# A fused attention, soft-MoE and MLP kernel: steps of the attention stage put at other places of the program

## The chip, the cores and the metric

The kernel runs on one core of a Trainium2 chip. A core has five engines, each with its own in-order instruction stream: TensorE (matmuls and transposes), VectorE, ScalarE, GpSimd and SyncE, whose queue here issues nearly all DMA transfers. Engines wait for each other by semaphores. The metric is the device time of one execution in microseconds (us), the median of the runs.

## What is computed

Rotary attention over 32 heads, a soft mixture of experts, and a gated MLP, all in 32 bit precision:

```python
def _attn_ref(q, k, v):                       # (4, 8, 576, 64)
    ...
    q_rot, k_rot = (rotate(q), rotate(k))
    scores = scale * np.matmul(q_rot, k_rot.transpose(0, 1, 3, 2))
    scores = scores - np.max(scores, axis=-1, keepdims=True)
    attn = np.exp(scores)
    attn = attn / (np.sum(attn, axis=-1, keepdims=True) + 1e-09)
    return np.matmul(attn, v).astype(np.float32)

def _moe_ref(x, phi, w1, w2):                 # x (2304, 512), 8 experts, 32 slots
    logits = x @ phi
    ...                                       # d: softmax over the tokens
    slot_input = d.T @ x
    ...                                       # two layers with relu for each expert's slots
    ...                                       # c: softmax of the logits over the slots
    return (c @ slot_out).astype(np.float32)

def _moe2_ref(x, w_in, w_out):                # 512 -> 2048 -> 512
    h = x @ w_in
    g = h * (1.0 / (1.0 + np.exp(-h)))
    return (g @ w_out).astype(np.float32)
```

## The kernel before

The kernel has an attention stage (up to about 361 us), the experts' two layers, and the MLP. The change is in the attention stage alone.

**Groups, pairs, places.** The 32 heads are taken as 16 pairs. A pair p has ten groups, numbered g = 10 p to 10 p + 9: for each half of the queries (288 of 576), five chunks of keys in the order 4, 0, 1, 2, 3. This text calls g - 10 p the place. In a group TensorE makes the scores of one chunk for both heads (L392/L393 at places 0 and 5, else L403/L404), ScalarE takes their exponential (L394, L405), and TensorE multiplies exponentials of the five groups before with the values (`pv`, L429, L432) at places 0 and 5, and at places 2 and 7 together with their sums (`sums`, L441, L443).

**The row maxima.** While pair p runs, nine units (L351) find the maxima of a later pair p + 2 from half-differences: TensorE makes two tiles `psmx`, ScalarE a relu (L356), VectorE a reduction (L365, into `mx`). A unit stands in each place except place 5: units 0 to 3 at places 6 to 9, units 4 to 8 at places 0 to 4 of the next pair. They need `kd`, the key difference (`k_diff`, L340, VectorE), and the operand tiles. When all nine are done, TensorE transposes `mx` (`max_rows`, L373, at place 5), ScalarE copies it (L378), and SyncE sends it into row 64 of `qb` (L379), which the scores of the pair need from its place 0 on.

**Rotary.** The queries and keys of a pair are loaded (`load`, L230), multiplied by the tables on VectorE (f0, L275) and GpSimd (f1, L278), added (f2, L281), rounded on ScalarE (f3, L285), and the rest subtracted (f4, L290), each once for both heads. SyncE then spreads the halves to the operand tiles: `m0` (three transfers, L294, waits for f3), `m1` (two, `sa` and `kb`, waits for f4), `m2` (L310, to `qb`).

**Batches of tokens.** Four pairs make a batch. Each pair's output `xt` (`norm2`, L461) is transposed in two parts (`x_t`, L473; ScalarE evicts them, L477 to L483), and a batch has the steps logits (L495), logits2 (L500), soft, expo (the exponential, L508), d_t (transposes L515 and copies L517/L518 into `d` and `lt`), s_mm (sums of the slots, L526/L529, copied by ScalarE, L530).

**PSUM.** `ps_st` has three buffers (scores, logits), `ps_mx` three (units), `ps_u` one (products), and `ps_m` one for the sums, the maxima, the transposes of x, d_t and s_mm in turn.

**Weights.** Loads of the experts' weights (`load_w`, L138) and the narrowing of the MLP's 64 bit weights go on beside it: `fetch` (L142) loads, `conv` narrows (ScalarE L152, VectorE L155, L158), `keep` (L653, L654) stores.

**What sets the order.** A table of tasks, filled by hand-set numbers. After the matmuls of a group, its tasks run in the order in which they were put in; a number is relative to the pair's first group, so -24 for pair p is place 6 of pair p - 3:

```python
for o, k, a in ROTARY:
    at(g0 + o[min(p, 5) - 2], rt(p, k, *a))
at(g0 + V_LOAD, lambda p=p: load_v(p))
first(g0 + (K_DIFF_2, K_DIFF_3, K_DIFF_4, K_DIFF)[min(p, 5) - 2], lambda p=p: k_diff(p))
...
at(g0 + X_T[p % 4][i], lambda p=p, i=i: x_t(p, i))
...
at(gc - FETCH_AHEAD, lambda i=i: fetch(i))
```

The order thus made is each engine's order; an engine does not wait for a group to end, only for the semaphores of its next instruction.

Of the kernel before, what the change touches and what calls it, by code (L numbers as in the profile page):

```python
# [38 lines left out]
ROT_2 = (-26, -22, -19, -21, -23, -19, -19, -18, -18, -18, -17, -18, -17)  # L39
ROT_3 = (-31, -25, -27, -26, -26, -24, -23, -23, -22, -16, -22, -19, -15)  # L40
ROT_4 = (-28, -28, -26, -28, -24, -23, -23, -20, -22, -17, -19, -21, -17)
ROT = (-31, -30, -30, -28, -26, -25, -24, -23, -22, -21, -22, -21, -20)
Q_COPY = -6
V_LOAD = -6
K_DIFF_2 = -14
K_DIFF_3 = -15
K_DIFF_4 = -16
K_DIFF = -17
QK_LOAD = -35
QK_LOAD_3 = -54  # L50
QK_LOAD_4 = -31
# [3 lines left out]
MAX_ROW_3 = -5  # L55
RECIP = 7
NORM = 7
X_T = ((21, 26), (16, 21), (16, 21), (16, 21))
W_IN_AT = (10, 20, 30, 40, 49, 60, 70, 81, 89, 100, 110, 120)
W_IN_STEPS = (1, 1, 5)  # L60
FETCH_AHEAD = 5
BATCH = (14, 16, 20, 21, 22, 23, 26, 30)
W_LOADS = (34, 54, 64, 75, 66, 84, 86, 76, 105, 95, 118, 130, 126, 143, 127, 137, 136, 138, 145, 155)
SCALES = -19
W_OUT_EARLY = (3, 6, 9, 12)
W_OUT_AT = ((0, 122, 130, 133), (1, 135, 139, 143))
# [10 lines left out]
def attn_softmoe_mlp_kernel(ctx: ExitStack, tc: tile.TileContext, qk, v, cst, phi, w1, w2, w_in, w_out, out):  # L77
# [119 lines left out]
    with tc.manual_schedule():  # L197
        with ExitStack() as t1:
# [37 lines left out]
            def load_v(p):  # L236
                t = (ops_c, p2)[p % 2].tile([128, 5, 128], F32, tag="v", bufs=1, name=f"v{p}")
                (act if p == NPAIR - 1 else sp).dma_start(out=t, in_=v[p])
                vt[p] = t
# [96 lines left out]
            def k_diff(p, heads=slice(0, 2)):  # L336
                ka = operands(p)[1]
                k = bass.AP(tensor=ka.tensor, offset=ka.offset, ap=[(W2, 128), (640, 2), (1, S)]).bitcast(F32)[:, heads]
                kd_of[p % 2] = p
                dve.tensor_tensor(out=kds[p % 2][:, heads], in0=k[:, :, 0:HS], in1=k[:, :, HS:S], op=ALU.subtract)  # L340
# [294 lines left out]
            def at(g, *fs):  # L635
                tasks.setdefault(g, []).extend(fs)

            def first(g, f):
                tasks.setdefault(g, []).insert(0, f)
# [23 lines left out]
            def rt(p, k, *a):  # L663
                return lambda: begin(p) if k == 8 else rot[p][k](*a)
# [3 lines left out]
            def begin_batch(b):  # L668
                bt[b] = batch(b)
# [3 lines left out]

            ROTARY = [([r[i] for r in (ROT_2, ROT_3, ROT_4, ROT)], k, a) for i, (k, a) in enumerate(((8, ()), (0, (0,)), (1, (0,)), (1, (1,)), (0, (1,)), (2, (0,)), (2, (1,)), (3, (0, act)), (3, (1, act)), (5, ()), (4, (0,)), (4, (1,)), (6, ())))]

            for p in range(NPAIR):
# [3 lines left out]
                if p >= 2:  # L680
# [4 lines that stand above are left out]
                if p >= 3:  # L685
# [12 lines left out]
                for i in range(2 * (p < NPAIR - 1)):  # L698
                    at(g0 + X_T[p % 4][i], lambda p=p, i=i: x_t(p, i))
                if p % 4 == 3 and p < NPAIR - 1:  # L700
                    b = p // 4
                    at(g0 + BATCH[0], lambda b=b: begin_batch(b), bf(b, 0, 0))
                    at(g0 + BATCH[1], bf(b, 0, 1))
                    at(g0 + BATCH[2], bf(b, 1, 0))
                    at(g0 + BATCH[3], bf(b, 1, 1))
                    at(g0 + BATCH[4], bf(b, 2))
                    at(g0 + BATCH[5], bf(b, 3))
                    at(g0 + BATCH[6], bf(b, 4))
                    at(g0 + BATCH[7], bf(b, 5))
            for i in range(12):  # L710
                gc = W_IN_AT[i]
                at(gc, lambda i=i: conv(i), lambda i=i: cv[i][0]())
# [23 lines left out]
            for i in range(NWA + 4):  # L736
                at(W_LOADS[i], lambda i=i: load_w(i))
            at(10 * NPAIR + SCALES, scales)
# [505 lines left out]
```

## Time and profile before

| | |
|---|---|
| runs | 629.95, 635.74, 639.93 us; median 635.74 |
| profiled execution | 634.98 us, of which the profile's span is 633.2 us |
| busy: TensorE, VectorE, ScalarE, GpSimd | 587.9, 407.0, 359.8, 233.6 us |
| mean granted clock of TensorE | 0.975 |
| DMA | 113.86 MB, mean 180 GB/s |

The profile is of one execution. PE is TensorE, PEld its weight loads (they overlap PE), DVE is VectorE, ACT ScalarE, POOL GpSimd, SP SyncE. A row of the timeline has start, duration, engine, line, operation, tiles (buffer numbers left out) and shapes, and in brackets the idle time of the engine before it and what ended it.

### The profile page before, as it was taken

The page shows a single profiled execution, that of the slowest core. Times are in us where ns is not written, and L with a number is a line of the kernel's source. Part 1 is how long each engine was busy: PE and PEld are TensorE (multiplying, and loading weights), DVE is VectorE, ACT ScalarE, POOL GpSimd, SP SyncE. Part 2 cuts the span into 40 slices and gives each one's busy share as a digit, 9 for nine tenths or more (in the row PEclk, how much of TensorE's full clock was granted, in tenths as well). Part 3 has the DMA queues.
Part 4 walks back from the last instruction along what each step waited for, and adds up shares of the span by engine and source line. Part 5 has one row for each costly group of instructions (what it writes and reads, how often), then busy time and mean ns, then how long its engine had stood idle before and what let it go on. Part 6 is the DMA issues. An engine that isn't in the chain of part 4 may idle for free.

```text
span 633.2 us, 10521 instructions
## 1 busy us (share of the span) xinstructions
PE 587.9 (93%) x3571; PEld 421.4 (67%) x3571; DVE 407.0 (64%) x865; ACT 359.8 (57%) x920; POOL 233.6 (37%) x195
## 2 busy tenths in 40 slices
PE   5768799999999999999989999799899999999997
PEld 3545467766676766765666434577788888888886
DVE  6687678888798887895643433678755544454452
ACT  3446467776776767775665331588664443444342
POOL 5365548767578566773453000312300000000000
PEclk9678889999999999998999999999999999999999
DMA  6885769977789986878959899734202000020002
GB/s 214 206 216 162 201 145 281 246 217 239 212 231 303 303 245 200 226 237 225 297 199 365 297 389 394 277 122 152 85 1 93 8 0 1 2 100 1 0 1 99
DMA packets 43188, 113.86 MB, mean 180 GB/s; under 512 B 4976, under 2 KB 6272, under 8 KB 41344
## 3 DMA queue, kind: packets, MB, share of 16 engines
q1 hardware_dynamic: 42956, 112.87, 58.3%
q8 instruction: 28, 0.46, 0.3%
q10 hardware_dynamic: 180, 0.34, 0.2%
q14 instruction: 24, 0.20, 0.1%
HBM read 78.12 MB, written 7.60 MB: 135 GB/s over the span
## 4 chain that ended last, share of the span: by engine, by line
PE 70%; ACT 11%; DVE 8%; DMA 7%; issue 3%; SPq 0%; POOL 0%; ACTq 0%; DVEq 0%
PE ops L1186 9%; PE ops L1184 9%; PE ops L1185 9%; PE u L432 8%; PE psmx L351 5%; PE st L403 4%; PE st L404 3%; PE s L441 3%; PE l L926 3%; DMA w_in_raw<-in_w_in_dram 3%; PE hps L1079 2%; PE u L429 2%; PE s L443 2%; PE l L905 2%; ACT e L405 2%
## 5 line engine op out<-in xcount | busy, mean ns | idle before, releaser
L405 ACT ACTIVATE e<-st 128x288 f32<-128x288 f32 x256 | 104.4, 419 | 30.3 <-PE st L404 27.6
L1184 PE MATMUL ops<-wo_hi,ghi 128*128 128x512 f32 x288 | 112.8, 392 | 0.0
L1186 PE MATMUL ops<-wo_hi,glo 128*128 128x512 f32 x288 | 112.4, 390 | 0.0
L1185 PE MATMUL ops<-wo_lo,ghi 128*128 128x512 f32 x288 | 112.4, 390 | 0.0
L1086 DVE TENSOR_TENSOR hps<-hps,g 128x384 f32<-128x384 f32 x96 | 49.8, 561 | 84.4 <-ACT g L1083 84.0
L1083 ACT ACTIVATE g<-hps 128x384 f32<-128x384 f32 x96 | 42.3, 490 | 81.9 <-PE hps L1079 81.6
L403 PE MATMUL st<-sa,sa 128*128 128x288 f32 x256 | 85.9, 337 | 0.2
L365 DVE CUSTOM_DVE_ANT_0 relu<-psmx,relu 128x288 f32<-128x288 f32 x144 | 64.4, 449 | 30.8 <-ACT relu L356 22.6
L417 POOL TENSOR_TENSOR es<-e,e 128x576 f32<-128x576 f32 x31 | 46.5, 1499 | 98.9 <-ACT e L405 98.9
L432 PE MATMUL u<-e,v 128*64 128x288 f32 x512 | 79.9, 430 | 0.0
L404 PE MATMUL st<-qb,kb 65*128 65x288 f32 x256 | 76.2, 299 | 0.0
L403 PEld LDWEIGHTS st<-sa,sa 128*128 128x128 f32 x256 | 49.2, 192 | 23.9 <-issue 14.9
L356 ACT ACTIVATE relu<-psmx 128x288 f32<-128x288 f32 x144 | 60.1, 420 | 8.6 <-PE psmx L351 6.2
L1186 PEld LDWEIGHTS ops<-wo_hi,glo 128*128 128x128 f32 x288 | 54.1, 188 | 11.4
L278 POOL TENSOR_TENSOR raw<-raw,tab 128x576 f32<-128x576 f32 x31 | 54.9, 1776 | 17.4 <-DMA sa<-sa 8.1
L1185 PEld LDWEIGHTS ops<-wo_lo,ghi 128*128 128x128 f32 x288 | 54.1, 188 | 10.0 <-issue 0.4
L1184 PEld LDWEIGHTS ops<-wo_hi,ghi 128*128 128x128 f32 x288 | 54.1, 188 | 9.9 <-issue 0.2
L432 PEld LDWEIGHTS u<-e,v 128*64 128x64 f32 x512 | 36.6, 141 | 31.3 <-issue 16.4
L351 PE MATMUL psmx<-sa,sa 128*128 128x288 f32 x160 | 48.3, 319 | 9.0 <-DVE mx L365 7.4
L422 POOL TENSOR_TENSOR es<-es,e 128x576 f32<-128x576 f32 x31 | 53.8, 1734 | 4.8 <-ACT e L405 3.5
L1092 DVE TENSOR_TENSOR glo<-hps,ghi 128x384 fp32r<-128x384 f32 x96 | 49.4, 551 | 4.9 <-ACT ghi L1089 1.8
L351 PE MATMUL psmx<-kd,sa 128*128 128x288 f32 x160 | 47.4, 313 | 5.2 <-DVE kd L340 4.1
(197 smaller groups left out, 1024.8 us busy)
## 6 DMA issues: line engine op xcount, KB each, us to landing
w<-in_w_dram SPq DMA_DIRECT2D x64, 512.0 KB
sa<-raw SPq DMA_DIRECT2D x56, 288.0 KB
raw<-in_qk_dram SPq DMA_DIRECT2D x13, 1152.0 KB
w_out_raw<-in_w_out_dram SPq DMA_DIRECT2D x16, 512.0 KB
w_in_raw<-in_w_in_dram SPq DMA_DIRECT2D x12, 512.0 KB
v<-in_v_dram SPq DMA_DIRECT2D x15, 320.0 KB
qb<-sa SPq DMA_DIRECT2D x16, 288.0 KB
out_dram<-os SPq DMA_DIRECT2D x18, 256.0 KB
```

Of the source, the lines that this page charges most:

```text
L278: eng.tensor_tensor(out=r[:, hd, 1], in0=r[:, hd, 1], in1=c(1), op=ALU.mult)
L351: pe.matmul(t, lhsT=rem_cols(qa, hd, 128) if u == 4 else qa[:, c0:c0 + 128], rhs=k, start=u != 4 or hd == 0, stop=u != 4 or hd == 1)
L356: act.activation(out=r, in_=t, func=ACTF.Relu)
L365: dve.tensor_tensor_reduce(out=r, in0=mxt.pop((p, u, 1)), in1=r, scale=1.0, scalar=-3.0e38, op0=ALU.add, op1=ALU.max, accum_out=mx[p][:, u ...
L403: pe.matmul(st, lhsT=ka[:, c0:c0 + 128], rhs=qa[:, o:o + HS], start=True, stop=False)
L404: pe.matmul(st, lhsT=kb[0:65, c0:c0 + 128], rhs=qb[0:65, S * hd + HS * h:S * hd + HS * h + HS], start=False, stop=True)
L405: act.activation(out=e[:, hd], in_=st, func=ACTF.Exp, scale=0.125)
L422: add(out=es[p, h], in0=es[p, h], in1=e, op=ALU.add)
L432: pe.matmul(u_ps[p, h][64 * hd:64 * hd + 64, :], lhsT=vt[p][:, c, 64 * hd:64 * hd + 64], rhs=e[:, hd], start=False, stop=c == 3, skip_grou ...
L1184: pe.matmul(t, lhsT=a, rhs=wo_hi[k], start=k == 0, stop=False)
L1185: pe.matmul(t, lhsT=a, rhs=wo_lo[k], start=False, stop=False)
L1186: pe.matmul(t, lhsT=b, rhs=wo_hi[k], start=False, stop=k == 15)
```

## The change

The diff changes numbers of the tables alone:

```diff
-ROT = (-31, -30, -30, -28, -26, -25, -24, -23, -22, -21, -22, -21, -20)
+ROT = (-31, -30, -30, -28, -26, -24, -24, -23, -21, -21, -20, -21, -20)
-V_LOAD = -6
+V_LOAD = -5
-K_DIFF = -17
+K_DIFF = -16
-X_T = ((21, 26), (16, 21), (16, 21), (16, 21))
-W_IN_AT = (10, 20, 30, 40, 49, 60, 70, 81, 89, 100, 110, 120)
+X_T = ((21, 26), (14, 21), (16, 19), (16, 20))
+W_IN_AT = (12, 20, 30, 40, 50, 58, 70, 81, 89, 100, 110, 120)
-BATCH = (14, 16, 20, 21, 22, 23, 26, 30)
-W_LOADS = (34, 54, 64, 75, 66, 84, 86, 76, ...)
+BATCH = (16, 16, 20, 21, 22, 25, 26, 29)
+W_LOADS = (34, 54, 64, 76, 66, 82, 86, 76, ...)
```

`ROT` and `K_DIFF` hold from pair 5 on. The entries of `ROT` are begin, f0 head 0, f1 head 0, f1 head 1, f0 head 1, f2 head 0, f2 head 1, f3 head 0, f3 head 1, m0, f4 head 0, f4 head 1, m1: f2 of head 0 and f3 of head 1 go one group later, f4 of head 0 two. `V_LOAD` holds from pair 2 on. `X_T` has the two parts of a batch's first to fourth pair. `BATCH` has, after logits of half 0 and 1, logits2 of half 0 and 1, soft, expo, d_t and s_mm. `W_IN_AT` has the groups in which twelve pieces are converted (the fetch is five groups earlier), `W_LOADS` those in which weight pieces 0 to 19 are loaded.

TensorE's order at places 4 to 6 of pair 10 shows the transposes `xps` of pairs 8 and 9, the first two of a batch (`st` are scores, the second number after the pair is the half, then the chunk or `r` for chunk 4, then the head). Before, at place 6:

```order
L373 MATMUL psm11_3088<-cst_sb_73,mx11_2841 9x128
L403 MATMUL st10_1_0_0_3102<-sa1_0_145,sa1_1_146 128x288
L404 MATMUL st10_1_0_0_3102<-qb0_152,kb1_150 128x288
L351 MATMUL psmx12_0_0_3106<-kd0_154,sa0_0_143 128x288
L403 MATMUL st10_1_0_1_3110<-sa1_0_145,sa1_1_146 128x288
L404 MATMUL st10_1_0_1_3110<-qb0_152,kb1_150 128x288
L351 MATMUL psmx12_0_1_3114<-sa0_1_144,sa0_0_143 128x288
L473 MATMUL xps8_1_3118<-cst_sb_73,xt8_2624 64x128
L473 MATMUL xps9_0_3121<-cst_sb_73,xt9_2894 128x128 x4
```

And now, at the end of place 4:

```order
L403 MATMUL st10_0_3_1_3063<-sa1_0_145,sa1_1_146 128x288
L404 MATMUL st10_0_3_1_3063<-qb0_152,kb1_150 128x288
L351 MATMUL psmx11_8_1_3067<-sa2_1_148,sa2_0_147 128x288
L473 MATMUL xps9_0_3071<-cst_sb_73,xt9_2894 128x128 x4
L392 MATMUL st10_1_r_3080<-sa1_0_145,sa1_1_146 128x288
```

The four transposes of pair 9 went from behind that of pair 8 to a place of their own.

VectorE's order in pair 1, places 2 to 4 (`relu2_4` is the reduction of unit 4 of pair 2, `hw0` and `w_in_32_0` belong to the first weight conversion, `raw4` is the rotary multiplication of pair 4). Before:

```order
L155 TENSOR_SCALAR w_in_32_0_583<-hw0_584 128x512
L158 SCALAR_TENSOR_TENSOR w_in_32_0_583<-w_in_raw0_475,w_in_32_0_583 128x512
L365 ISA relu2_4_613,mx2_540<-psmx2_4_1_619,relu2_4_613 128x288
L365 ISA mx2_540 128x1
L454 SCALAR_TENSOR_TENSOR s0_1_627<-s0_1_627,r00_1_633 128x288
L455 SCALAR_TENSOR_TENSOR rs0_1_632<-s0_1_627,r00_1_633 128x288
L461 SCALAR_TENSOR_TENSOR xt0_521<-u0_1_577,rs0_1_632 128x288
L275 TENSOR_TENSOR raw4_561<-raw4_561,tab_142 128x576
L365 ISA relu2_5_652,mx2_540<-psmx2_5_1_658,relu2_5_652 128x288
L365 ISA mx2_540 128x1
L365 ISA relu2_6_664,mx2_540<-psmx2_6_1_666,relu2_6_664 128x288
L365 ISA mx2_540 128x1
```

And now:

```order
L365 ISA relu2_4_608,mx2_540<-psmx2_4_1_614,relu2_4_608 128x288
L365 ISA mx2_540 128x1
L454 SCALAR_TENSOR_TENSOR s0_1_622<-s0_1_622,r00_1_628 128x288
L455 SCALAR_TENSOR_TENSOR rs0_1_627<-s0_1_622,r00_1_628 128x288
L461 SCALAR_TENSOR_TENSOR xt0_519<-u0_1_577,rs0_1_627 128x288
L275 TENSOR_TENSOR raw4_561<-raw4_561,tab_142 128x576
L365 ISA relu2_5_650,mx2_540<-psmx2_5_1_656,relu2_5_650 128x288
L365 ISA mx2_540 128x1
L365 ISA relu2_6_662,mx2_540<-psmx2_6_1_664,relu2_6_662 128x288
L365 ISA mx2_540 128x1
L155 TENSOR_SCALAR w_in_32_0_640<-hw0_641 128x512
L158 SCALAR_TENSOR_TENSOR w_in_32_0_640<-w_in_raw0_523,w_in_32_0_640 128x512
```

The conversion went behind the normalization (L454 to L461), the rotary multiplication and the reductions of units 4, 5 and 6.

SyncE's order around the row maxima of pair 2 (`m2` into `qb0`), from the value load `v2` on; `raw3` goes to the operand tiles `sa0`, `kb0`, and `raw5` is the load of pair 5, which takes the buffer of `raw3`. Before:

```order
L238 DMA v2_693<-in_v_dram 128x640
L294 DMA sa0_1_144<-raw3_326 64x2x576 x2
L294 DMA sa0_0_143<-raw3_326 64x2x576 x2
L294 DMA kb0_149<-raw3_326 64x2x576
L230 DMA raw5_715<-in_qk_dram 128x2304
L653 DMA w_in0_88<-w_in_32_0_583 128x128
L654 DMA w_in_32_0_91<-w_in_32_0_583 128x384
L142 DMA w_in_raw1_719<-in_w_in_dram 128x1024
L379 DMA qb0_152<-m2_740 1x9x128
```

And now:

```order
L294 DMA sa0_1_144<-raw3_326 64x2x576 x2
L294 DMA sa0_0_143<-raw3_326 64x2x576
L238 DMA v2_711<-in_v_dram 128x640
L294 DMA sa0_0_143<-raw3_326 64x2x576
L294 DMA kb0_149<-raw3_326 64x2x576
L230 DMA raw5_715<-in_qk_dram 128x2304
L142 DMA w_in_raw1_717<-in_w_in_dram 128x1024
L379 DMA qb0_152<-m2_738 1x9x128
L653 DMA w_in0_88<-w_in_32_0_640 128x128
```

Three of the operand transfers went ahead of the value load, and the two stores of the converted weights went behind the row maxima. In pairs 5 to 15 the key difference (L340) stands on VectorE behind the reduction of unit 8 instead of ahead of it.

## Rows read from the trace of the kernel before

**Rows 1.** The page's busy time and share of the span, TensorE first
```profile
PE 587.9 (93%) x3571; PEld 421.4 (67%) x3571; DVE 407.0 (64%) x865; ACT 359.8 (57%) x920; POOL 233.6 (37%) x195
```

**Rows 2.** Stretches: length, PE, PEld, DVE, ACT, POOL busy, clock, DMA share, GB/s
```profile
260.00:280.00 20.00, 19.91 (x141) 14.74 (x141) 18.01 (x42) 15.57 (x44) 16.29 (x13) 1.00 0.90 243
```

**Rows 3.** TensorE's waits, 100 to 356 us: in all, times, longest
```profile
PE xps L473 <- ACT x L477: 1.5, 1, 1.5
PE st_r L393 <- DMA qb<-m: 1.4, 1, 1.4
PE xps L473 <- ACT x L483: 1.3, 2, 0.7
PE psm L373 <- DVE mx L365: 1.3, 4, 0.7
PE s L441 <- DVE lt L518: 1.0, 2, 0.5
PE s L441 <- ACT x L480: 1.0, 2, 0.5
PE lgh L566 <- DVE xt L461: 0.6, 1, 0.6
```

**Rows 4.** TensorE's waits, 26 to 125 us
```profile
PE psmx L351 <- DVE mx L365: 7.4, 2, 5.6
PE st_r L393 <- DMA qb<-m: 3.2, 2, 2.8
...
PE xps L473 <- ACT x L483: 0.6, 1, 0.6
```

**Rows 5.** Timeline of all engines, 58 to 65 us (pair 1, places 2 to 4)
```profile
58.64 1.78 DVE L158 SCALAR_TENSOR_TENSOR w_in<-w_in_raw,w_in 128x512 uint32<-128x512 uint32 x1
59.60 0.44 ACT L450 ACTIVATE r<-rs 128x288 f32<-128x288 f32 x1
...
60.71 0.45 DVE L454 SCALAR_TENSOR_TENSOR s<-s,r 128x288 f32<-128x288 f32 x1
...
62.00 1.40 POOL L278 TENSOR_TENSOR raw<-raw,tab 128x576 f32<-128x576 f32 x1
62.13 1.88 DVE L275 TENSOR_TENSOR raw<-raw,tab 128x576 f32<-128x576 f32 x1
63.94 0.44 DVE L365 CUSTOM_DVE_ANT_0 relu<-psmx,relu 128x288 f32<-128x288 f32 x1
...
64.45 0.40 PE L351 MATMUL psmx<-sa,sa 128*128 128x288 f32 x1 [1.86 <-DVE mx L365]
```

**Rows 6.** Stretches after two idle times of TensorE, columns as in rows 2
```profile
65.90:69.30 3.40, 3.40 (x12) 1.29 (x12) 1.26 (x3) 0.41 (x1) 0.75 (x1) 0.50 0.81 184
79.50:82.90 3.40, 3.40 (x13) 1.54 (x12) 1.97 (x4) 1.32 (x3) 0.31 (x1) 0.50 0.37 79
```

**Rows 7.** Timeline of all engines, 261 to 264.2 us (pair 11, places 4 to 6)
```profile
261.53 0.75 DVE L340 TENSOR_TENSOR kd<-sa 128x576 fp32r<-128x576 f32 x1
261.63 1.91 POOL L278 TENSOR_TENSOR raw<-raw,tab 128x576 f32<-128x576 f32 x1
262.58 1.58 DVE L275 TENSOR_TENSOR raw<-raw,tab 128x576 f32<-128x576 f32 x1
263.51 1.94 POOL L422 TENSOR_TENSOR es<-es,e 128x576 f32<-128x576 f32 x1
...
264.00 0.30 PE L351 MATMUL psmx<-kd,sa 128*128 128x288 f32 x1
```

**Rows 8.** Timeline of all engines, 74 to 79 us (pair 1 place 9, pair 2 place 0)
```profile
74.73 2.75 DVE L281 TENSOR_TENSOR raw<-raw 128x576 f32<-128x576 f32 x2
77.40 0.44 DVE L365 CUSTOM_DVE_ANT_0 relu<-psmx,relu 128x288 f32<-128x288 f32 x1
...
78.39 0.40 ACT L356 ACTIVATE relu<-psmx 128x288 f32<-128x288 f32 x1
...
78.85 0.40 PE L351 MATMUL psmx<-sa,sa 128*128 128x288 f32 x1
```

## What the change was predicted to do

> **What bounds the kernel now.** I read the engines' busy time first, then the stretches, then what the bounding engine waited for. TensorE is busy for 93% of the span [rows 1], and in a calm stretch of the attention stage it is busy for 19.91 us of 20 at full clock while VectorE has 18.01 and ScalarE 15.57 [rows 2]. So a moved instruction of another engine is worth only the TensorE wait that it ends or makes. From 100 to 356 us the rows of these waits add up to 8.1 us [rows 3]; of the earlier, rougher part the rows that matter are three [rows 4]. That is nearly all that a new order can give back there, because the diff removes no work: each engine has the same instructions as before.
>
> I count places 0 to 9 inside a pair's ten groups (place 4 of pair 10 is group 104).
>
> **The change part by part.**
>
> *Transposes of a batch's first two pairs.* Before, the last transpose of a batch's first pair and the first four of its second stand at one place and share the one buffer of `ps_m`, so the second set waits until ScalarE has emptied the first. That is the 0.6 of pair 2 [rows 4], the two waits of 1.3 in pairs 6 and 10 and the 1.5 of pair 14 [rows 3]. Now the second set stands two places earlier, behind place 4, alone. Its input is done just before (VectorE writes it in the same place), so I leave no new wait there, at worst 0.1 each. Gain 0.6 + 1.3 + 1.5 = 3.4; in pair 14 the sums behind it want the same buffer, which ScalarE empties as late as before, so I take 1.2 of the 1.5: 3.1 us, bounds 2 and 3.4.
>
> *Sums of the batch's slots one place earlier.* ScalarE's copy of them now comes before it evicts the transposes of place 1. Before it came behind, was late, and made the softmax sums wait for `ps_m` (two waits, 1.0 [rows 3]). Gain 0.9, bounds 0 and 1.0.
>
> *Batch exponential two places later, one rotary addition one later.* The exponential no longer stands ahead of the last reductions of a pair; the copies of the transposed logits come on VectorE ahead of a rotary addition instead of behind it. The latter ends the wait of the sums for `lt` (two, 1.0 [rows 3]): 0.9, bounds 0 and 1.0. The former, with the key difference moved behind the ninth reduction, ends the wait for `mx` (four, 1.3 [rows 3]). The largest of these, 0.7 in pair 8, I don't count: there a weight conversion on VectorE makes the reduction late, and the key difference, now last, will be waited for instead. Gain 0.6, bounds 0 and 1.3.
>
> *The key difference behind the reduction, in all pairs from the fifth.* This is where the change can lose. Now it starts at 261.53 and takes 0.75, just ahead of GpSimd's multiplication at 261.63, which is held up (1.91) [rows 7]. After, the reduction (0.45) goes first, so it would start near 262.25, in the middle of that multiplication. The next VectorE instruction shows what this costs: started at 262.58 in the same GpSimd instruction, it ended at 264.16, 0.62 after GpSimd's end at 263.54 [rows 7]. GpSimd's own, no longer held up, needs 1.40 [rows 5], so it ends at 263.03 and the key difference at 263.65. TensorE first reads it at 264.00 [rows 7]. Spare 0.3: cost 0. If GpSimd's instruction took its 1.91 still, it would end at 264.16 and cost 0.2 in each of eleven pairs, 2.2 us; that is the upper bound.
>
> *First weight conversion two places later (pair 1).* It takes 1.78 us on VectorE from 58.64 and pushes the normalization to 60.71, though ScalarE's reciprocal was there at 60.04 [rows 5]. What follows slides behind GpSimd's instruction at 62.00: the rotary multiplication then takes 1.88, the reduction behind it ends at 64.38, and TensorE, which wants its buffer, resumes at 64.45 after 1.86 idle [rows 5]. With the conversion behind two more reductions the chain starts 0.6 earlier, the multiplication gets in ahead of GpSimd's at 62.00 and takes between 0.75 and 1.2, and the wait shrinks to some 0.3. That is 1.5 us. Right behind it the clock is at half [rows 6], and work that comes earlier runs more in that stretch, so I take 1.3, bounds 0 and 3.
>
> *Loads of values one place later.* In SyncE's queue the value load of pair 2, which waits for TensorE, no longer stands ahead of three operand transfers of pair 3; so pair 5's big load and behind it the row maxima of pair 2 go out sooner. TensorE waits 2.8 for these maxima at the start of pair 2 [rows 4]. I count 0.1 for it, for another wait lies under it: VectorE's two rotary additions hold it until 77.48, its reduction ends at 77.84, ScalarE's at 78.79, and TensorE's matmul that needs both came at 78.85, hardly later than it had to [rows 8]. When the maxima are in time, TensorE will wait there for VectorE and ScalarE.
>
> *Rotary steps and operand transfers.* The second rounding goes one place later, the lower half's subtraction two. So SyncE sends a pair's operand transfers later, the last two by up to the 1.58 that one VectorE instruction takes beside GpSimd's [rows 7]. No row from 100 us on shows TensorE waiting for them [rows 3], and the units that read them stand five places on: cost 0, and no more than that lateness per pair if it is wrong.
>
> *Logits, single transposes, weight loads.* The first logits move two places down, next to the second; TensorE does the same matmuls. They take two of the three `ps_st` buffers in a row, which ScalarE empties while TensorE is at the sums and products of place 7: cost 0, without that cover one eviction more to wait for in each of three batches, about the 0.44 of ScalarE's reciprocal, which has as many elements [rows 5]. The single transposes of a batch's third and fourth pair find `ps_m` free at their new places: 0. Weight loads that pass others in SyncE's queue (in pair 8 one goes ahead of `qb` and the maxima) are hidden as long as the maxima land before the next pair begins: 0, else what pair 13 shows, 1.4 once [rows 3].
>
> *The last pair.* The transposes of pair 14 leave the way of the last reciprocal; the wait of 0.6 for the last normalized half [rows 3] goes: 0.6, bounds 0 and 0.6.
>
> *Where it is tighter.* In pairs 6 and 10 the rounding now stands behind the copy of the slot sums, for which ScalarE waits, and VectorE's subtraction and the reductions stand behind the rounding: 0.2 each. In pair 5 a conversion on ScalarE (now at place 0) comes between the logits and the exponentials: 0.3. Together 0.7, bounds 0 and 2. The wait of 1.4 for `qb` in pair 13 [rows 3] stays: the early output weights that hold up SyncE's queue there aren't touched.
>
> **Sum.** 3.1 + 0.9 + 0.9 + 0.6 + 1.3 + 0.1 + 0.6 - 0.7 = 6.8 us. The profiled execution took 634.98, so 628.2; the median of the runs is 635.74, so near to it that I leave the number at 628.2 us.
>
> **The rivals.**
> 1. *Each ended wait uncovers the next*, as at the start of pair 2. Transposes, sums and eviction lie within 1 us of each other, so some 5 of the 6.8 may be gone: 633 us. For it speaks that rows 8 shows just this; against it, that the floor is known: the calm stretch, which has the same matmuls, has 0.09 us idle in 20 [rows 2].
> 2. *The key difference loses to two GpSimd instructions.* If GpSimd's next one (1.94 at 263.51 [rows 7]) took its turn before VectorE's, the key difference would end near 263.03 + 1.40 + 0.75 = 265.2, 1.2 after TensorE wants it; in eleven pairs 13 us, so 641 us. It decides from 0.6 us in each pair on (6.8 / 11), where the gain is eaten. Against it: VectorE's waiting instruction got in at 263.54 although GpSimd's next was there at 263.51 [rows 7]. The Trainium skill ("SBUF — State Buffer", Who interferes with whom) has it that a VectorE instruction with two SBUF inputs and a GpSimd one that reads SBUF exclude each other for the whole instruction, whoever comes first; it says nothing of who is next. By that rule the trace agrees: the 0.75 became 1.58 for a like instruction that came second.
> 3. *The clock.* From 65.90 and from 79.50 TensorE had half its clock, 1.2 instead of 2.4 GHz, for 3.40 us each, busy all through [rows 6], after idle times of 1.86 and 2.8. If the first stretch doesn't come, because pair 1 has less idle time, that is up to 1.7 us; if the earlier maxima help after all and the second goes too, 3.4: 624.8 us. The Trainium skill ("TensorE: Matmul & The Clock Gate", What's actually happening) puts it that throttled is the default and activity releases the clock; which idle time is enough no run here shows yet.
>
> **How the numbers follow.** My forecast 0.5, rival 1 0.22, rival 2 or late operand transfers 0.13, rival 3 0.15. The bounds of the parts, added, give 621 (all gains, no cost, clock kept) to 639; I take 621 to 637, which leaves out the far end of rival 2. The likeliest case alone runs from 625 to 631. Faster by over 2%, which is about what a measurement of this kernel can tell from no change, means under 623.0: only the far end of rival 3, 0.1. Slower by over 2% is above 648.5, which no case reaches: 0.02. Within 2%: 0.88.
>
> **What would show it.** Right: among TensorE's waits those of `xps` for `x` gone, those of the sums for `lt` and `x` gone, no wait of `psmx` for `kd`, the wait in pair 1 under 0.5; the wait for `qb` at the start of pair 2 replaced by one for `mx` or a reduction. Wrong: a wait of `psmx` for `kd` or for an operand transfer in every pair, or the same total under other names.

## The result and the profile after

The changed kernel took 623.3 us (median of four runs, 621.59 to 626.74) beside 633.55 for the kernel before, a ratio of 0.985 (95% interval 0.981 to 0.989). Six further runs, taken together with three of the experiments, have a median of 627.5 beside 634.5 for the kernel before, a ratio of 0.989 (0.984 to 0.993). The ten runs of the changed kernel together have a median of 626.7. So the change makes the kernel 1.1 to 1.5% faster, some 7 to 10 us; 628.2 was forecast, 6.8 less than the profiled execution of before, and 621 to 637 was the range. Here and below the medians are of all executions, while the ratios and intervals leave out those more than 1.5% above the fastest of their kernel (among them five of the twelve with the transposes alone, the profiled one too).

The first profile after is of the fastest of these runs, 621.59 us with a span of 619.8. Its page, in the columns of [rows 1]:

```profile
PE 579.9 (94%) x3571; PEld 418.7 (68%) x3571; DVE 398.0 (64%) x865; ACT 360.9 (58%) x920; POOL 228.9 (37%) x195
```

The instructions are as many as in [rows 1]. TensorE is busy 8.0 us less for the same work, VectorE 9.0 and GpSimd 4.7: less of TensorE's time was at half clock, and VectorE's and GpSimd's instructions are shorter, as they are where the two don't meet.

TensorE's waits from pair 3 on, 91.8 to 335.6 us, columns as in [rows 3]:

```profile
PE st L403 <- ACT e L405: 2.3, 6, 0.7
PE st_r L393 <- DMA qb<-m: 2.3, 2, 1.4
PE psmx L351 <- DMA sa<-raw: 1.5, 2, 0.9
PE s L441 <- ACT x L477: 0.4, 2, 0.2
```

Against [rows 3]: every wait of `xps`, of `psm` for `mx`, and of `s` for `lt` is gone, and there is none for `kd` in this profile. Three kinds are new or larger: for exponentials (L405), for `qb`, for operand transfers. From 26 to 91.8 us, against [rows 4]:

```profile
PE psmx L351 <- DVE mx L365: 4.0, 1, 4.0
PE psmx L351 <- DMA sa<-raw: 3.9, 2, 2.4
...
PE st_r L393 <- DMA qb<-m: 0.7, 2, 0.4
```

Two things must be kept apart from here on. The first profile is not alone: a second one of the same kernel was taken (below), and the two differ mostly in pairs 0 to 2. The lengths in this table are read from the traces, from the first L392 of pair 0 to that of pair 3, and from there to the start of pair 15's last group. Each is of one execution.

| kernel | pairs 0 to 2 | from pair 3 on |
|---|---|---|
| before | 71.1 | 249.1 |
| after, first and second profile | 65.2, 70.0 | 243.7, 245.1 |
| before + transposes | 71.7 | 253.1 |
| before + rotary and key difference | 70.2 | 252.4 |
| before + batch steps | 70.3 | 245.3 |
| before + conversions and weight loads | 66.8 | 251.5 |
| before + value loads | 73.1 | 249.0 |
| before + transposes, conversions later | 69.8 | 255.0 |
| after, rotary and key difference back | 69.4 | 246.0 |
| after, conversions later | 71.2 | 249.5 |
| after, queue put right | 71.1 | 242.1 |
| after, words earlier | 70.4 | 245.0 |
| after, queue and words | 66.1 | 240.8 |

What comes behind is not quite the same either: from the start of pair 15's last group to the end of the span it is 286.1 us before, 284.3 and 286.8 in the two profiles after.

### The profile page after: what moved, and what is told of

Read it like the earlier page. It is cut to its first block, busy times and chain, and to the rows that moved or that the text cites. A ratio compares the mean times of both kernels' runs of the same rounds, so it can differ in the third digit from the quotient of the medians.

```text
span 619.8 us, 10519 instructions
## 1 busy us (share of the span) xinstructions
PE 579.9 (94%) x3571; PEld 418.7 (68%) x3571; DVE 398.0 (64%) x865; ACT 360.9 (58%) x920; POOL 228.9 (37%) x195
## 5 line engine op out<-in xcount | busy, mean ns | idle before, releaser
L405 ACT ACTIVATE e<-st 128x288 f32<-128x288 f32 x256 | 102.8, 419 | 27.5 <-PE st L404 25.2
L417 POOL TENSOR_TENSOR es<-e,e 128x576 f32<-128x576 f32 x31 | 48.9, 1578 | 90.6 <-ACT e L405 90.5
L432 PE MATMUL u<-e,v 128*64 128x288 f32 x512 | 76.6, 416 | 0.0
L356 ACT ACTIVATE relu<-psmx 128x288 f32<-128x288 f32 x144 | 59.8, 418 | 11.1 <-PE psmx L351 10.4
L278 POOL TENSOR_TENSOR raw<-raw,tab 128x576 f32<-128x576 f32 x31 | 50.7, 1639 | 17.5 <-DMA raw<-in_qk_dram 12.9
L422 POOL TENSOR_TENSOR es<-es,e 128x576 f32<-128x576 f32 x31 | 50.6, 1632 | 6.1 <-ACT e L405 4.8
```

The costliest lines, as they stand in the source:

```text
L278: eng.tensor_tensor(out=r[:, hd, 1], in0=r[:, hd, 1], in1=c(1), op=ALU.mult)
L356: act.activation(out=r, in_=t, func=ACTF.Relu)
L405: act.activation(out=e[:, hd], in_=st, func=ACTF.Exp, scale=0.125)
L422: add(out=es[p, h], in0=es[p, h], in1=e, op=ALU.add)
L432: pe.matmul(u_ps[p, h][64 * hd:64 * hd + 64, :], lhsT=vt[p][:, c, 64 * hd:64 * hd + 64], rhs=e[:, hd], start=False, stop=c == 3, skip_grou ...
```

## The experiments

All change numbers of the tables alone; where the transfer of words is placed by itself, `FETCH_AHEAD` becomes a list of groups, `FETCH`.

**The parts one at a time.** Four parts of the diff were put into the kernel before, each alone: the line of `X_T`, the lines of `ROT` and `K_DIFF`, those of `W_IN_AT` and `W_LOADS`, and that of `V_LOAD`.

> The kernel before with the change's places of the transposes alone (X_T). By the prediction's step: the waits of `xps` for `x` in pairs 2, 6, 10 and 14 are gone and the time falls by 3.1 us (bounds 2 and 3.4), that is by 0.5%. In the changed kernel place 6 of pairs 6 and 10 went from 2.24 to 0.91 us while place 4, where the four transposes stand now, went from 0.81 to 1.16; so pairs 6 and 10 should each be 1.0 shorter, pair 2 too, pair 14 some 0.9: 3.9 us. By the rival (each ended wait uncovers the next) the waits change their names only, the pairs keep 20.6 us, and the time stays.

> The kernel before with the change's rotary steps and key difference alone (ROT and K_DIFF). By the prediction's step this is worth nothing, at worst 0.2 in each of eleven pairs lost. By the rival that the two traces suggest, it shortens place 0 of pairs 3 to 13 from 3.23 to 2.86 us each: before, VectorE's subtraction for the lower half (L290) stood ahead of the reduction that frees TensorE's buffer for the next unit; two places later it doesn't. That is 0.37 in eleven pairs, 4.1 us. The operand transfers and so the big load and the words of the weights come later too: in pairs 3, 7 and 11 ScalarE's conversion then waits for the words and place 2 goes from 3.08 to 3.8, 2.1 lost. Net 2 us less by the rival, 0 to 2.2 more by the step.

> The kernel before with the change's places of weight conversions and weight loads alone (W_IN_AT and W_LOADS). By the prediction's step: the idle time of 1.86 us in pair 1 shrinks to some 0.3 and the time falls by 1.3 us (bounds 0 and 3); the weight loads cost nothing. By the rival, which the changed kernel's trace suggests: the 1.86 goes, but TensorE then waits at place 6 of pair 1 for the operand transfers of pair 3, which do not come sooner, some 1 to 2 us, so that pair 1 keeps its 25 us within 0.7; and at the start of pair 9 there is a wait of 0.9 for `qb`, for a weight load now stands ahead of the row maxima. Sum by the rival: 0 to 1 us more.

> The kernel before with the change's place of the value loads alone (V_LOAD). By the prediction's step: 0.1 us less, place 0 of pair 2 keeps some 7 us, since under the wait for the row maxima lie VectorE's two rotary additions, 2.75 us beside GpSimd. By the rival that the trace of the changed kernel suggests: the additions are late for the same reason as the maxima or meet GpSimd only because TensorE was late; with the maxima there in time place 0 of pair 2 falls from 7.27 to some 4.3, and the half-clock stretch that followed the idle time (3.4 us from 79.53) goes, so 3 to 5 us less.

Then the line of `BATCH` alone:

> The kernel before with the change's batch steps alone (BATCH: first logits two places down, exponential two later, sums of the slots one earlier). By the prediction's steps: the waits of the sums for `x` and `lt` (0.5 each, four) and those of `psm` for `mx` (1.3 in all) go, some 2 us less (0.9 + 0.9 + 0.6 and a loss of up to 0.4 where the rounding stands behind the copy). By the rival that the three runs of single parts suggest: the pairs lose their waits, but TensorE, sooner at places 0 and 2 of the pairs in which ScalarE narrows a piece of the words of a weight (pairs 3, 4, 7, 8, 11, 12), finds ScalarE waiting there for the transfer of that piece, and gives 2 us or more back: no change within 2 us.

| part alone | ratio to before | 95% interval |
|---|---|---|
| transposes | 0.998 | 0.995 to 1.001 |
| rotary and key difference | 1.003 | 1.000 to 1.005 |
| conversions and weight loads | 1.003 | 1.001 to 1.006 |
| value loads | 0.998 | 0.996 to 1.000 |
| batch steps | 0.998 | 0.996 to 1.000 |

No part is worth more than 1.5 us by itself. Only two are clear of the noise: the conversions and weight loads lose, the value loads just gain. The five add up to nothing (-0.1%; their intervals together leave some 0.6% either way), while all together give 1.1 to 1.5%. The profiles show pieces of the reason, place by place.

*Transposes alone.* Place 6 of pairs 6 and 10 fell from 2.24 to 0.92 and place 4 rose from 0.81 to 1.16, as expected; pairs 6 and 10 are 1.0 shorter. But in this profile, of an execution of 639.7 us, pairs 3 and 7 are 5.3 and 3.7 us longer, at place 2, where TensorE waits 2.16 and 1.39 for exponentials and half clock follows. That the shorter executions of this kernel have such long pairs too is not shown.

*What holds the exponentials* is best seen in the run of the conversions alone, pair 4, where place 2 went from 3.71 to 7.70 (rows of ScalarE and TensorE):

```profile
116.56 0.66 ACT L152 ACTIVATE hw<-w_in_raw 128x512 f32<-128x512 f32 x1 [4.26 <-DMA w_in_raw<-in_w_in_dram]
117.57 0.40 PE L403 MATMUL st<-sa,sa 128*128 128x288 f32 x1 [2.48 <-ACT e L405]
```

ScalarE had stood 4.26 us at a conversion whose words had not landed; behind it in its order are the exponentials. Half clock followed for 3.4 us from 118.4, which takes the rest. The run of the rotary steps alone has such a wait in pair 4 too (2.0 idle).

*Rotary and key difference alone.* Place 0 fell from 3.23 to 2.86 in calm pairs, as the rival had it. Its cost did not come where the rival put it: place 2 of pairs 3, 7 and 11 stayed at 3.08 to 3.09, and ScalarE had the words there within 0.4 us of wanting them. The key difference cost something here that it does not in the whole change. VectorE's and TensorE's rows of pair 5:

```profile
146.25 1.40 POOL L422 TENSOR_TENSOR es<-es,e 128x576 f32<-128x576 f32 x1
146.45 1.82 DVE L340 TENSOR_TENSOR kd<-sa 128x576 fp32r<-128x576 f32 x1
...
148.33 0.40 PE L351 MATMUL psmx<-kd,sa 128*128 128x288 f32 x1 [0.70 <-DVE kd L340]
```

It came second to GpSimd, by 0.20, and took 1.82: 0.70 lost in pairs 5 and 9, and place 6 of pairs 3, 7 and 11 went from 1.25 to 1.52.

*Conversions alone.* Pair 1 lost its idle 1.86 and got 2.69 at place 6 for operand transfers, more than the rival had said; pair 2's place 0 fell from 7.27 to 4.38, which neither theory gave to this part. Pair 9 had no wait for `qb`.

*Value loads alone.* This is what the prediction said, to the name of the wait: place 0 of pair 2 took 7.07 (7.27 before), and TensorE's 2.8 for `qb` [rows 4] is now one for the reduction behind VectorE's two additions:

```profile
74.47 2.76 DVE L281 TENSOR_TENSOR raw<-raw 128x576 f32<-128x576 f32 x2
75.00 1.61 POOL L422 TENSOR_TENSOR es<-es,e 128x576 f32<-128x576 f32 x1 [0.26 <-POOL es L420]
77.66 0.53 PE L351 MATMUL psmx<-kd,sa 128*128 128x288 f32 x2 [2.28 <-DVE mx L365]
```

*Batch steps alone.* The best part: 3.8 us from pair 3 on. TensorE's waits there, 96.9 to 342.4 us, among others:

```profile
PE psm L373 <- DVE mx L365: 2.0, 4, 1.4
...
PE s L441 <- DVE lt L518: 1.0, 2, 0.5
```

The waits of `s` for L480 are gone; those for `lt` stay, since the rotary addition that ends them was not moved. The expected loss at the conversions (2 us) did not come. Of the 3.8, some 1.7 are pair 13, which kept its wait for `qb` but not the half clock behind it.

**The conversions two places later.** In two kernels ScalarE's conversions of pairs 3, 4, 7, 11 and 12 went behind the exponentials of place 2, with the transfers where they were (two weight loads, which take a buffer that comes free later, went two groups later with them):

```diff
-W_IN_AT = (12, 20, 30, 40, 50, 58, 70, 81, 89, 100, 110, 120)
+W_IN_AT = (12, 20, 32, 42, 50, 58, 72, 81, 89, 100, 112, 122)
-FETCH_AHEAD = 5
+FETCH = (7, 15, 25, 35, 45, 53, 65, 76, 84, 95, 105, 115)
```

> The changed kernel with five of the weight conversions (of pairs 3, 4, 7, 11 and 12) two places later, at place 2 instead of place 0, their transfers in the same places as before (and two weight loads two groups later, since they take a buffer that comes free later). If the waits for exponentials at place 2 (0.2 to 0.7 each in the profile, and place 2 itself 0.7 to 1.2 longer in pairs 3, 7, 11 and 12) come from ScalarE standing at a conversion whose words aren't there, they go: pairs 3, 7, 11 and 12 some 0.7 shorter each, 3 us less in all. If they come from ScalarE's work as such, they stay or come elsewhere, for the conversion still takes 0.7 of ScalarE: 0 to 1 us less.

> The kernel before with the transposes' places of the change (as in the first run) and, besides, five weight conversions two places later, their transfers where they were. The transposes alone shortened pairs 6 and 10 by 1.0 each as expected but brought no time, since pairs 3 and 7 became 3.7 to 5.3 longer: ScalarE stood 3 to 4 us at a conversion that waited for its words, and the exponentials behind it were late. If that is what eats the gain, then with the conversions behind the exponentials of place 2 the gain of 3 to 4 us remains (ratio 0.994 to 0.995). If the transfers themselves are what is short, pairs 3 and 7 stay long under another wait, and the time is that of before.

The first is slower than the changed kernel, 0.996 of before (0.993 to 0.999); the second is slower than before, 1.010 (1.007 to 1.014). Place 2 was cured in both, as expected: 3.08 to 3.12 us in pairs 3, 7 and 11. But a conversion has VectorE's half too. Pair 7 of the second kernel, on VectorE and TensorE:

```profile
186.04 1.67 DVE L340 TENSOR_TENSOR kd<-sa 128x576 fp32r<-128x576 f32 x1
187.63 1.62 DVE L155 TENSOR_SCALAR w_in<-hw 128x512 uint32<-128x512 uint32 x1
189.28 0.69 DVE L158 SCALAR_TENSOR_TENSOR w_in<-w_in_raw,w_in 128x512 uint32<-128x512 uint32 x1
189.89 0.45 DVE L365 CUSTOM_DVE_ANT_0 relu<-psmx,relu 128x288 f32<-128x288 f32 x1
...
190.41 0.28 PE L373 MATMUL psm<-cst_sb,mx 128*9 128x128 f32 x1 [2.56 <-DVE mx L365]
```

The 3.9 us from L340 to L158 now stand ahead of the last reduction, and the transpose of the maxima waits 1.7 to 2.6 for it in each of the five pairs (0.5, and 1.0 behind it, in the first kernel). So the waits at place 2 did come from ScalarE standing at conversions whose words were late, and the later place was no cure.

**SyncE's queue ahead of the row maxima.** In the changed kernel:

```diff
-W_LOADS = (34, 54, 64, 76, 66, 82, 86, ...)
+W_LOADS = (34, 54, 64, 76, 66, 84, 86, ...)
-W_OUT_AT = ((0, 122, 130, 133), (1, 135, 139, 143))
+W_OUT_AT = ((0, 126, 132, 135), (1, 135, 139, 143))
```

> The changed kernel with three numbers of SyncE's queue put back or on: the weight load that went from group 84 to 82 back to 84, and the early output weights of pair 12 fetched at place 6 instead of 2 (narrowed two groups later), behind the row maxima. By the theory that the row maxima of pairs 9 and 13 are late because of the loads ahead of them: the waits for `qb` at the start of pairs 9 (0.88) and 13 (1.40) go, place 0 of these pairs falls from 4.4 and 4.9 to some 3.0, 3 us less. By the rival (the transfers as a whole are what is short; what comes first delays the next): the wait goes to `sa<-raw` or to ScalarE's words, and less than 1 us is gained.

624.9 us, 0.983 of before (0.979 to 0.988). Place 0 of pairs 9 and 13 is 3.28 in both (4.39 and 4.90 in the first profile after). That these loads alone hold the maxima up is not shown: the first kernel with later conversions and the one with earlier words (below) keep the load at 82, and pair 9 has no wait for `qb` in either; pair 13 has none or little (3.28 and 3.75) with the early output weights where they were. From pair 3 on it is 242.1 us long, 1.5 and 3.0 less than the two profiles of the changed kernel. TensorE's waits there have no `qb` any more:

```profile
PE st L403 <- ACT e L405: 3.0, 5, 1.2
PE psmx L351 <- DMA sa<-raw: 1.2, 1, 1.2
PE psm L373 <- DVE mx L365: 0.6, 1, 0.6
```

Its first groups, up to group 82, have the order of the changed kernel, but pairs 0 to 2 took 71.1 us, not 65.2. Hence the next run.

**The changed kernel again, the words earlier, both, and the rotary steps back.** The words of four conversions go out one group earlier, which puts them ahead of the value load, the maxima and the big load:

```diff
-FETCH_AHEAD = 5
+FETCH = (7, 15, 24, 35, 45, 53, 64, 76, 84, 95, 104, 114)
```

> The changed kernel itself, a second profile of it beside more runs on the same chip as the next three. Two theories of the 5.9 us that the changed kernel's first profile gained before pair 3 (71.1 us for pairs 0 to 2 before, 65.2 after). If they are the change's (the conversion behind the normalization), this profile has 65 to 66 again, and the ratio is 0.985. If they are one of two outcomes of the same order (another kernel with the same order up to group 82 took 71.1 there, with 34 us at half clock instead of 20), the runs spread over some 6 us, and a profile shows either; what belongs to the change is then the part from pair 3 on, 5.5 us in the first profile.

> The changed kernel with four transfers of a conversion's words (for the conversions at groups 30, 70, 110 and 120) issued one group earlier, so that in SyncE's queue they stand ahead of the pair's value load, the row maxima and the big load. If the waits at place 2 of pairs 3, 7, 11 and 12 (place 2 is 0.6 to 1.2 longer than in pairs 4 and 10) come from late words, place 2 falls to 3.1 in all four, 2.5 to 3 us less, unless the row maxima or the operands are late instead: then the start of the next pair or place 6 gets a wait of 1 us or more and nothing is gained. Theory: 2 us less; rival (the transfers as a whole are short): within 0.5 us of the changed kernel.

> The kernel with the queue put right at the starts of pairs 9 and 13 (weight load back to 84, early output weights two to four groups later) and, besides, the four transfers of words one group earlier. If the two add up: place 0 of pairs 9 and 13 at 3.3 (from 4.4 and 4.9) and place 2 of pairs 3, 7, 11, 12 at 3.1, some 5 us less than the changed kernel from pair 3 on, 618 us where the first 70 us are alike. If one wait takes the place of another: 622 to 624.

> The changed kernel with the rotary steps and the key difference put back (ROT and K_DIFF as before). If they are worth 0.37 at place 0 of pairs 3 to 13, as the run of them alone showed, place 0 goes back from 2.86 to 3.23 in these pairs and this costs 4.1 us; the words come sooner, which gives back up to 2.5 at place 2 of pairs 3, 7, 11, 12: 1.5 to 4 us slower than the changed kernel from pair 3 on. By the prediction's step (they are worth nothing): the time of the changed kernel.

| kernel | median us | ratio to before | 95% interval |
|---|---|---|---|
| changed kernel again | 627.5 | 0.989 | 0.984 to 0.993 |
| words earlier | 624.9 | 0.986 | 0.982 to 0.990 |
| queue and words | 625.0 | 0.982 | 0.978 to 0.987 |
| rotary steps and key difference back | 629.5 | 0.992 | 0.989 to 0.995 |

*Again.* Pairs 0 to 2 took 70.0 us: pair 0 is 2.2 longer than in the first profile, pair 2 is 3.0 longer, and pair 1 is 0.5 shorter. What can differ between two executions is seen at places 3 and 4 of pair 1, where VectorE's multiplication and GpSimd's meet. First profile, then second:

```profile
58.77 0.75 DVE L275 TENSOR_TENSOR raw<-raw,tab 128x576 f32<-128x576 f32 x1
58.89 1.90 POOL L278 TENSOR_TENSOR raw<-raw,tab 128x576 f32<-128x576 f32 x1
```

```profile
62.41 1.42 POOL L278 TENSOR_TENSOR raw<-raw,tab 128x576 f32<-128x576 f32 x1
62.46 1.98 DVE L275 TENSOR_TENSOR raw<-raw,tab 128x576 f32<-128x576 f32 x1
...
64.87 0.40 PE L351 MATMUL psmx<-sa,sa 128*128 128x288 f32 x1 [1.32 <-DVE mx L365]
```

By 0.12 us VectorE was first in the one, by 0.05 GpSimd in the other, and TensorE's next unit waits 1.32 us there. (The first profile loses 2.44 at place 6 instead, so pair 1 does not gain by it.) The same happens to the additions at the start of pair 2 (2.62 for the two beside GpSimd in the second profile, 1.42 in the first, where both began ahead of GpSimd's next).

*Words earlier.* Place 2 is 2.99 to 3.09 in pairs 3, 7, 11 and 12 and ScalarE has the words 4 to 6 us before it wants them. Some of it comes back: VectorE's half of the conversion, now sooner, delays a reduction at place 4 (0.72 in pairs 3 and 7), and the words of pair 4's conversion, which stayed behind in the queue, are later (place 2 there 4.52 instead of 2.99). From pair 3 on: 245.0 us, no gain. *Both*: 240.8 us, the shortest; the ratio is the lowest too, by less than the intervals tell apart. Against the changed kernel on the same chip the median is 2.5 us lower, with intervals that overlap; from pair 3 on, the traces show 2.8 to 4.3 us.

*Rotary back.* Place 0 is at 3.20 to 3.22 again in calm pairs, the waits for `lt` (1.0) and one of 1.4 for `mx` in pair 8 are back. From pair 3 on it is 1.0 to 2.4 longer than the changed kernel. So by the traces these steps are a gain within the whole, where they gained nothing alone; the times agree in sign (629.5 and 627.5), but their intervals overlap.

## Why the prediction was right, and where it was not

**The total** was near (626.7 over ten runs, 628.2 said), with gains and costs both counted too small, and with a clock that adds or takes several us. That it was so near is in part luck: a gain of 2.6 us at place 0 and a loss of 3.2 at place 2 (below) were not in the sum and nearly cancel in the first profile, and pairs 0 to 2 alone differ by 4.7 us between two profiles of the same kernel.

**Transposes (3.1).** Right at the places themselves, somewhat small, but not in what follows: pairs 2, 6 and 10 lost 1.0 each at places 4 and 6, pair 14 0.9 at places 4 to 7, 3.8 together, above the bound of 3.4. The step priced the listed wait (0.66); TensorE's own time at the two places shows 1.33 less and 0.35 more. "No new wait" fails one pair later: the ended wait at place 6 had been time for the words of the next pair's conversion (see the late words, below).

**Slot sums, `lt`, `mx` (0.9, 0.9, 0.6).** All these waits went. Moving the sums to place 9 costs 1.44 there in pairs 5, 9 and 13 and gives 1.69, 1.69 and 1.41 at place 0 of the next pair and 0.54 at place 2 of pairs 6 and 10: 1.6 net, where 0.9 was said. With the rotary steps back the waits for `lt` are back, so that term is shown to belong to the addition. In pair 8 the second profile shows the key difference waited for (0.65), as the step said.

**Key difference (0).** Right to the hundredth. Pair 11 after, beside [rows 7]:

```profile
251.91 1.41 POOL L278 TENSOR_TENSOR raw<-raw,tab 128x576 f32<-128x576 f32 x1
252.46 1.47 DVE L340 TENSOR_TENSOR kd<-sa 128x576 fp32r<-128x576 f32 x1
253.28 1.94 POOL L422 TENSOR_TENSOR es<-es,e 128x576 f32<-128x576 f32 x1
254.22 0.30 PE L351 MATMUL psmx<-kd,sa 128*128 128x288 f32 x1
```

It ended at 253.93, 0.61 after GpSimd's 253.32 (0.62 in [rows 7]) and 0.29 before TensorE read it; 0.3 was the spare. Rival 2 (641) falls: GpSimd's next did not go ahead. The run of this part alone shows how thin the spare was.

**Rotary and operand transfers (0).** The step that failed most: nothing was said, and there was a gain. At place 0, before, then after (pair 11):

```profile
252.13 0.70 ACT L285 ACTIVATE raw<-raw 128x576 fp32r<-128x576 f32 x1
252.95 0.43 PE L351 MATMUL psmx<-kd,sa 128*128 128x288 f32 x2
252.99 0.43 ACT L356 ACTIVATE relu<-psmx 128x288 f32<-128x288 f32 x1
253.48 0.30 PEld L351 LDWEIGHTS psmx<-sa,sa 128*128 128x128 f32 x2 [0.33 <-ACT relu L356]
253.48 0.53 PE L351 MATMUL psmx<-sa,sa 128*128 128x288 f32 x2
```

```profile
242.30 0.44 ACT L356 ACTIVATE relu<-psmx 128x288 f32<-128x288 f32 x1
242.83 0.43 PE L351 MATMUL psmx<-kd,sa 128*128 128x288 f32 x2
242.88 0.73 ACT L285 ACTIVATE raw<-raw 128x576 fp32r<-128x576 f32 x1
243.10 0.42 PE L351 MATMUL psmx<-sa,sa 128*128 128x288 f32 x2
```

Before, ScalarE's second rounding (L285) stood ahead of the relu (L356) that empties the buffer TensorE wants next, and the second two matmuls began 0.53 after the first two; now the relu goes first, and they begin 0.27 after. With the restart behind the gap (0.53 for two matmuls, 0.42 now) this is 0.37 a pair, 2.6 us in seven pairs. (Not VectorE's subtraction, as the expectation for the rotary steps alone had it: TensorE resumes 0.06 after the relu's end, whereas the reduction behind the subtraction has only just begun.) TensorE's matmuls are idle for only 0.10 there (253.38 to 253.48), and no row of [rows 3] has it. The list of TensorE's weight loads did have it, 100 to 356 us before, and not after:

```profile
PEld psmx L351 <- ACT relu L356: 3.0, 9, 0.3
```

It is gone with the rotary steps alone, too, and with them put back into the changed kernel it is back, seven times. Besides, operand transfers were waited for in pair 8 (0.9) and pair 13 (0.6) of the first profile; the latter is there (0.5) with the rotary steps back as well.

**The late words (in no term).** In the changed kernel ScalarE gets the words 1.5 to 2 us late in pairs 3, 7, 11 and 12, and place 2 is 0.6 to 1.2 longer in each, 3.2 us (4.3 in the second profile). SyncE sends them behind the row maxima. Pair 11 before, then after:

```profile
245.82 0.80 SPq L379 DMA_DIRECT2D qb<-m  x1
247.66 0.43 SPq L142 DMA_DIRECT2D w_in_raw<-in_w_in_dram  x1
```

```profile
237.06 0.80 SPq L379 DMA_DIRECT2D qb<-m  x1
238.89 0.43 SPq L142 DMA_DIRECT2D w_in_raw<-in_w_in_dram  x1
245.83 0.68 ACT L152 ACTIVATE hw<-w_in_raw 128x512 f32<-128x512 f32 x1 [1.62 <-DMA w_in_raw<-in_w_in_dram]
246.86 0.40 PE L403 MATMUL st<-sa,sa 128*128 128x288 f32 x1 [0.22 <-ACT e L405]
```

Both times the words go out 1.84 or 1.83 us after the maxima. But place 6, where the maxima go out, has lost TensorE's wait for the transposes, and so pair 11 begins 3.31 us after the words are sent (242.20) and not 4.67 (252.32). The other traces show which part does that:

| kernel | words sent before pairs 7, 11 begin | place 2 of pairs 7, 11 |
|---|---|---|
| before | 4.68, 4.67 | 3.09, 3.08 |
| rotary and key difference alone | 4.09, 4.65 | 3.09, 3.08 |
| transposes alone | 3.34, 3.31 | 6.65, 3.29 |
| after, first profile | 3.80, 3.31 | 3.79, 3.80 |
| after, rotary and key difference back | 3.80, 3.32 | 3.09, 3.31 |

Most of the lead goes with the transposes; the rotary steps alone take 0.6 of it in pair 7 and none in pair 11, and putting them back gives none of it back. (No run put the transposes alone back.) How long the words then take to land varies too, in pair 7 from 6.3 us (rotary steps back) over 7.4 and 8.9 (changed kernel) to 8.5 (transposes alone); what sets that is open. With the rotary steps TensorE comes to place 2 another 0.37 sooner and feels the lateness more. In pair 3 the transposes shorten the lead too (3.21 before, 2.54 after, 2.66 with the rotary steps back). In pair 12, where no wait of `xps` ended, it is 2.97 with the rotary steps moved or back (3.67 before): there the big load ahead of the words waits 0.7 and 1.0 for operand transfers to land, and which part brings that on is open.

**First conversion (1.3).** The chain came as described: in the first profile the multiplication was ahead of GpSimd's, took 0.75, and the idle time of 1.86 [rows 5] was gone. But 2.44 came two places later for the operand transfers of pair 3, which the prediction held free, and pair 1 is only 0.7 shorter. In the second profile the same order lost the meeting by 0.05 us, and pair 1 is 1.1 shorter all the same: the size was near, with other waits than those described.

**Maxima of pair 2 (0.1).** Right for the value loads: 0.2 alone. The 3.0 that place 0 of pair 2 lost in the first profile go with the moved conversion (2.9 lost with that part alone) where VectorE gets ahead of GpSimd; in the second profile place 0 took 7.20 again, with a wait of 2.03 for `mx` in place of that for `qb`, which is what the prediction said.

**Weight loads (0, else 1.4 once).** The second half of the sentence came true: a load went ahead of the maxima in pair 8, and pair 9 waits 0.88 for `qb` (0.40 in the second profile). The wait is gone with the load put back, though other moves end it too (above). Pair 13's 1.4 stayed, as said, but it too goes in other orders that leave the early output weights alone: with the rotary steps alone there is none.

**The last pair (0.6).** The wait of 0.61 went, and went with the transposes alone as well; the last matmul of these logits starts 1.08 sooner after pair 15's last group begins (8.00 instead of 9.08). It is not always kept. In five of the nine profiles with moved transposes, the second of the changed kernel among them, a stretch of half clock of 3.4 us begins some 13 us after that group, and the MLP begins 57.1 us after it, not 55.4; before it was 56.5. None of the five profiles with the transposes unmoved has the stretch.

**Where it is tighter (-0.7).** Pair 5 lost 0.5 and 0.3 at place 1 in the two profiles (0.3 was said), with the conversion alone 0.4; in pairs 6 and 10 places 0 to 3 show no such loss.

**The clock (rival 3).** Means over the execution: before, then the first profile after, then the second.

```profile
core 0: 633.2 us, clock 0.975
```

```profile
core 0: 619.8 us, clock 0.983
```

```profile
core 0: 628.3 us, clock 0.972
```

The rival came about in the first profile, not in the second. How loose it is, the wait for `qb` in pair 13 shows: 1.41, 1.40 and 1.58 us. The stretches right behind it, before, first, second (columns as in [rows 2]):

```profile
291.20:294.60 3.40, 3.40 (x13) 1.56 (x12) 1.04 (x3) 0.62 (x2) 0.00 (x0) 0.51 0.72 211
```

```profile
280.80:284.20 3.40, 3.40 (x22) 2.27 (x23) 1.49 (x4) 0.98 (x3) 0.00 (x0) 1.00 0.58 189
```

```profile
286.30:289.70 3.40, 3.40 (x13) 2.33 (x14) 1.14 (x3) 0.82 (x2) 0.00 (x0) 0.52 0.57 205
```

Thirteen matmuls at 1.2 GHz against 22 at 2.4 in the same time; place 0 of the pair took 6.50, 4.90 and 6.64.

**Rival 1** is partly true: in pair 1 an ended wait uncovered the next, and the ended waits of the transposes uncovered that for the words in pairs 3, 7 and 11.

**What stays open.** Why the parts alone add up to nothing is shown in pieces (the key difference's waits without the batch steps, the waits for `lt` without the rotary addition, words that come late once the transposes' waits are gone, with half clock behind), but these pieces are of single profiles and don't make up the whole difference. What sends pairs 0 to 2 into 65 or 71 us was not isolated. Whether the kernel with queue and words beats the changed one is not settled by its times.

## What to carry to other kernels

Before ending a wait, ask what had used its time: here transfers that go out at a fixed distance behind the row maxima lost 1.3 us of lead, and an in-order engine then stood at their landing with other work behind it. Read the waits of TensorE's weight loads beside those of its matmuls, and starts of matmuls against each other: nine waits of 0.33 in the one list were gaps of 0.1, too short for the other, and seven of them cost 0.37 each. When a run puts a part in or takes it out, look whether the cost goes with it before giving it to that part. And where two engines' instructions meet within 0.1 us, carry both outcomes as two times; one profile shows only one of them.

## What the runs showed of the hardware

- A VectorE and a GpSimd instruction on two inputs of 128x576 that meet took 2.01 to 2.03 us from the start of the first to the end of the second in the places shown here, whichever went first: VectorE, second, ended 0.61 or 0.62 after GpSimd's end (in four places: 253.93, 148.27 and 64.44 above, and [rows 7]); GpSimd, second, ended 1.27 after VectorE's (60.79, 59.52). In all fourteen traces, of 707 such VectorE instructions (L275, L281, L290, L340) that began inside one of GpSimd's (L278, L417, L422), 706 ended 0.6 to 0.7 after it, and of 549 GpSimd instructions that began inside VectorE's, 539 ended 1.3 after it (alone they take 0.75 and 1.40). So VectorE, waiting, came ahead of GpSimd's next. What the order decides is which engine's next work waits.
- The same program, pairs 0 to 2: 65.2 and 70.0 us. The landings of its transfers in the first 35 us lie up to 1.7 us apart (TensorE's wait for an operand transfer in pair 0 was 1.49 and 2.30), and the meetings and the clock differ from there on; that the landings are the cause is an inference.
